# B's masks as a minimum on VectorE, early weights, held-back broadcasts and new planner weights in a two-part attention kernel

## Chip, cores, metric

One core of a Trainium2 chip runs the whole program in one launch. The metric is the device time of one execution in microseconds. Eight executions of the kernel before took 404.08 to 408.78 us, median 406.32.

## What is computed

Two independent attention layers over 2048 positions of 448 features, 16 heads of 28, concatenated:

```python
# A: one key/value head shared by 16 query heads, full softmax
q = (x @ wq).reshape(B, S, H, Dh).transpose(0, 2, 1, 3); k = x @ wk; v = x @ wv
p = softmax(einsum("bhqd,bkd->bhqk", q, k) * Dh ** -0.5)
a = einsum("bhqk,bkd->bhqd", p, v).transpose(0, 2, 1, 3).reshape(B, S, H * Dh) @ wo
# B: each position sees itself and 7 earlier ones at distance 2, 4, ..., 14
idx = pos[:, None] - arange(8)[None, :] * 2; mask = idx >= 0
logits = where(mask, einsum("bhsd,bhswd->bhsw", q, kg) * scale, -1e9)
b = (einsum("bhsw,bhswd->bhsd", softmax(logits), vg)).transpose(0, 2, 1, 3).reshape(B, S, D) @ wo
out = concatenate([a, b], axis=-1)
```

## The kernel before

A python planner (`plan`, `loop`) keeps a clock for each engine, asks for the next piece of work of the engine that is furthest behind, and writes down the instruction order of all five engines. Its costs, due times and thresholds are the constants at the head of the file. The program then runs those orders; a semaphore stands wherever an instruction needs another engine's result. So each engine runs strictly in the planned order, whatever the chip's true durations are.

**A.** The queries go by 16 groups (four chunks of 512 positions, four sets of four heads); each group has 64 jobs (16 blocks of 128 keys, four heads). A job is one QK matmul (`do_qk`, L1467) into a PSUM bank. Two rings of banks, three and two wide, alternate: ScalarE takes a ring with one exponential of 1536 or 1024 columns (L1214). Some jobs go by VectorE instead: a drain (`dread`, L1514) writes the score as an integer whose bits are a bf16 power of two, and two shifts (L1522, L1529), on VectorE or POOL, add three shifted copies that the PV products weigh. When no flexible bank is free, a job can be taken out of a three-wide ring. PV products (`do_pv`, L1577) run four at a time on column tiles of the array.

**B.** The positions are split by parity and half into four chunks, so that distance 2 becomes 1. Band matmuls of 32 keys by 25 queries (`b_fill`, L1310) write a bank; before them, four matmuls per bank (L1300) add a mask of 0 or -1e9 from `mask` through the identity. ScalarE takes each bank with one exponential (L1331), 16 in all; `bpv` (L1272) makes the PV products. Keys, queries and values come from `wB` and the transposed input `xT_B` (L654); values go through a scratch tensor in DRAM (`v_scratch`) into bands of 32.

**Fills.** Everything but QK and PV (projections, B's band matmuls, output projections) is a "fill", done in the order of its due time when TensorE has room before the next QK. `BT0` and `BDT` set B's due times. A dummy matmul is put in where TensorE would be too idle over a window (`HAMLOW`).

**Close of a group.** `chain` copies the PV bank (L980), moves the denominators by DMA, takes reciprocals (L996), writes them to DRAM, broadcasts them to 128 partitions with four DMAs on SP (`d3`), and multiplies on POOL (L1026). A's very last group is done on VectorE alone with two 32x32-block transposes (L950 to L971). When four groups of a chunk are ready, `outproj` runs 16 matmuls per 128 positions (`woA`, `woB`), copies the bank out (L1080 on ScalarE, L1082 on VectorE) and sends it by DMA.

**Start.** A's x chunk 0 is transposed on TensorE (L674); chunks 1 to 3 come by twelve DMA transposes on SP. Chunk 0's q (L654 on `wq`), its norm (a square on ScalarE, `sel`, an addition on VectorE, L755), k and v stand before the first QK. POOL builds constants and the mask, then issues the mask's copies, `wB` (as soon as k of chunk 0 is evicted), `woA` and `woB` (behind k of chunks 1 and 2). One DMA transpose of B's input is issued for every second exponential from the fourth on.

**Instruction fetch.** The planner assumes that TensorE's instructions arrive in blocks of 256 (`FBLOCK`, `block`, `fetched`) and keeps short matmuls away from a block that has not arrived.

Of the kernel before, what the change touches and what calls it, by code (L numbers as in the profile page):

```python
# [21 lines left out]
NEG = -1.0e9  # L22
# [35 lines left out]
BT0 = 98  # L58
BDT = 36
# [24 lines left out]
HAMLOW = 0.7  # L84
HAMTILE = 0.55
LATE = 1000.0
RINGD = 0.22
RINGB = 900.0
PRESS = 1
# [3 lines left out]
XL0 = 3600.0  # L93
FILLN = 130.0
FILL0 = 0.0
FRATE = 0.036

# [96 lines left out]
class _Gen:  # L194
# [297 lines left out]
    def plan_start(self):  # L492
# [29 lines left out]
        wA("act", g.wq, g.A_wq, D, "wq", 3800.0)  # L522
# [38 lines left out]
        for k in range(4):  # L561
# [6 lines left out]
                                     base=DH - 1, pattern=[[32, 4]], channel_multiplier=-1), 200, reads=[res("f2")], writes=[res("sel4")])  # L568
        gp(lambda e: e.memset(g.wB[0:64, 3, :], 0.0), 900, writes=[res("wB0")])
# [5 lines left out]
        gp(lambda e: e.memset(g.mask[0:32, :, :], 0.0), 450, writes=[res("m0")], name="band")  # L575

        def band(v, c0, n, rep, lo, rd, wr):
# [3 lines left out]
            gp(lambda e: e.affine_select(out=v, in_=v, compare_op=ALU.is_ge, fill=NEG, base=-lo, pattern=[[0, rep], [-1, n]],  # L581
                                         channel_multiplier=1), 270 + 2.0 * n * rep, reads=[rd], writes=[mid], name="band")
            gp(lambda e: e.affine_select(out=v, in_=v, compare_op=ALU.is_ge, fill=NEG, base=lo + HALO, pattern=[[0, rep], [1, n]],
# [6 lines left out]
        for s in range(1, 4):  # L590
            self.dma_op("gp", g.mask[32 * s:32 * s + 32, :, :], g.mask[0:32, :, :], reads=mres, writes=[res("mq", s)], issue=700.0, name="mq")
        self.mres = mres + [res("mq", s) for s in range(1, 4)] + [res("id")]
# [8 lines left out]
    def load_late(self, what):  # L601

        g = self
        res = self.res

        def dma(out, in_, reads, wr):
            def mk(eng, ns):
                return dict(dma=True, out=out, in_=in_, reads=reads, writes=[wr], lands=9000.0, moves=500.0)
            self.later(("gp",), (700,), reads, mk, prio=0, name="w")
        if what == 0:  # L610
            rd = [res("kA", 0), res("wB0")]
            dma(g.wB[:, 0:3, :], g.B_wqkv[0:384, :].rearrange("(k p) c -> p k c", p=128), rd, res("wB", 0))
            dma(g.wB[64:128, 3, :], g.B_wqkv[384:448, :], rd, res("wB", 1))
        else:
            t, src, key = ((g.woA, g.A_wo, "woA"), (g.woB, g.B_wo, "woB"))[what - 1]
            for j in range(4):
                dma(t[32 * j:32 * j + DH, :, :], src.rearrange("(t j d) c -> j d t c", j=4, d=DH)[j], [res("kA", what), res(key + "0")], res(key, j))

    def load_xb(self, exp):
# [9 lines left out]
        def mk(eng, ns):  # L629
            return dict(dma=True, transpose=True, out=g.xT_B[:, kt, 512 * c:512 * c + 512], in_=src, reads=[tick],  # L630
                        writes=[self.res("xB", c, kt)], lands=5500.0, moves=2000.0)
# [26 lines left out]
    def make_fills(self):  # L658
# [35 lines left out]
        for c in range(4):  # L694
# [7 lines left out]
            def after(bank, c=c):  # L702
# [3 lines left out]
                if c == 0:  # L706
                    self.evict(bank, lambda e: e.activation(kdst, ksrc, ACT.Identity, bias=g.col[:, 0:1]), ("act",), (480,),
                               reads=[res("c0")], writes=[res("kA", 0)], prio=0.5, name="ke", cb=lambda o: self.load_late(0))
# [3 lines left out]
                           prio=0.5 if c == 0 else 1, name="ke", cb=lambda o: self.load_late(c) if c < 3 else None)  # L712
# [143 lines left out]
        for b in range(16):  # L856
# [22 lines left out]
            fill(f"vB{b}", BT0 - 62 + 2.4 * b, steps, after, elig=30.0)  # L879
# [35 lines left out]
    def chain(self, key, bank):  # L915
# [93 lines left out]
        def d3(p, rk):  # L1009
# [6 lines left out]
            self.later(("sp",), (560,), [res("rd", rk)], mk, prio=0, gate=lambda: len(self.bcs.free) > 0, name="d3")  # L1016
# [111 lines left out]
    def loop(self):  # L1128
        guard = 0
        while self.nout < 32:  # L1130
            guard += 1
# [40 lines left out]
    def slot_free(self, slots, eng):  # L1172
        return len(slots.free) > 0 and self.ready(eng, [], [slots.res[slots.free[0]]]) <= self.T[eng] + 15.0

# [22 lines left out]
    def act_choose(self):  # L1197
# [3 lines left out]
        if self.actq:  # L1201
# [3 lines left out]
            if self.pslots.free and max(self.ready("act", [self.banks[b].res], []) for b in banks) <= T + 15.0:  # L1205
# [15 lines left out]
                if self.xbt and self.nexp >= 3 and self.nexp % 2 == 0:  # L1221
                    self.load_xb(op)
                return
# [66 lines left out]
    def b_fill(self, gg, j):  # L1290
# [5 lines left out]
        def steps(bank):  # L1296
            def mask(e):
                r = slice(32 * j, 32 * j + 32)
                for c in range(4):
# [470 lines left out]
```

## Time and profile before

| what | us |
|---|---|
| profiled execution, its own time | 404.08 |
| its span, first to last instruction | 402.3 |
| median of eight executions | 406.32 |
| ScalarE busy, of it A's exponentials (L1214) | 384.0, 371.6 |
| VectorE, POOL busy | 346.8, 130.0 |
| first exponential starts / last one ends | 10.49 / 389.80 |

The page gives for each engine the time in which it had an instruction, then groups of equal instructions with their count, busy time, mean length and the idle time before them. TensorE's matmuls overlap, so its busy share says less than the others'. The chain of waits follows the last instruction back to what released it. DMA queues: q1 is SP's, q10 ScalarE's, q0 POOL's, whose descriptors software writes; all share 16 DMA engines.

### The profile page before, as it was taken

The page shows a single profiled execution, that of the slowest core. Times are in us where ns is not written, and L with a number is a line of the kernel's source. Part 1 is how long each engine was busy: PE and PEld are TensorE (multiplying, and loading weights), DVE is VectorE, ACT ScalarE, POOL GpSimd, SP SyncE. Part 2 cuts the span into 40 slices and gives each one's busy share as a digit, 9 for nine tenths or more (in the row PEclk, how much of TensorE's full clock was granted, in tenths as well). Part 3 has the DMA queues.
Part 4 walks back from the last instruction along what each step waited for, and adds up shares of the span by engine and source line. Part 5 has one row for each costly group of instructions (what it writes and reads, how often), then busy time and mean ns, then how long its engine had stood idle before and what let it go on. Part 6 is the DMA issues. An engine that isn't in the chain of part 4 may idle for free.

```text
span 402.3 us, 16636 instructions
## 1 busy us (share of the span) xinstructions
PE 385.7 (96%) x7281; PEld 135.3 (34%) x7281; DVE 346.8 (86%) x803; ACT 384.0 (95%) x371; POOL 130.0 (32%) x165
## 2 busy tenths in 40 slices
PE   8897999999999999999999999999999999999995
PEld 4322222332233433222344333343333233333332
DVE  4886798889999999878999999899998878999832
ACT  3997999999999999999999999999999999999983
POOL 8830012733101021686101366420226611042510
PEclk9999999999999999999999999999999999999999
DMA  7699566424000022100001121100121210022404
GB/s 156 117 187 144 124 148 134 97 64 92 2 26 12 18 85 65 56 2 20 19 7 30 33 63 52 29 6 7 32 73 41 78 32 15 16 74 75 103 25 150
DMA packets 42532, 25.20 MB, mean 63 GB/s; under 512 B 28348, under 2 KB 37996, under 8 KB 42460
## 3 DMA queue, kind: packets, MB, share of 16 engines
q1 hardware_dynamic: 40332, 21.05, 23.3%
q0 software_dynamic: 736, 2.20, 2.9%
q8 instruction: 57, 0.93, 1.0%
q10 hardware_dynamic: 1392, 0.89, 0.8%
q14 instruction: 15, 0.12, 0.1%
HBM read 13.80 MB, written 6.02 MB: 49 GB/s over the span
## 4 chain that ended last, share of the span: by engine, by line
ACT 74%; PE 17%; DVE 5%; DMA 3%; issue 0%
ACT P L1214 72%; PE ps L1577 5%; PE ps L1467 4%; PE ps L654 3%; DMA xT_B<-in_B_x_dram 3%; DVE Z L1514 2%; ACT P L1331 1%; PE ps L1272 1%; PE ps L1310 1%; PE ps L596 1%; DVE Z L1529 1%; PE ps L674 0%; PE ps L1300 0%; DVE sq L1082 0%; DVE Z L1522 0%
## 5 line engine op out<-in xcount | busy, mean ns | idle before, releaser
L1214 ACT ACTIVATE P<-ps 128x1536 bf16<-128x1536 f32 (+1 forms) x341 | 371.6, 1271 | 4.6 <-PE ps L1467 4.5
L1514 DVE TENSOR_SCALAR Z<-ps 128x512 int16<-128x512 f32 x215 | 146.6, 686 | 20.0 <-PE ps L1467 18.7
L1577 PE MATMUL ps<-Z,vA 128*32 128x512 bf16 x860 | 143.8, 385 | 0.9 <-ACT P L1214 0.6
L1577 PE MATMUL ps<-P,vA 128*32 128x512 bf16 x809 | 139.0, 386 | 1.4 <-ACT P L1214 1.2
L1467 PE MATMUL ps<-qT_A,kT_A 29*128 29x512 bf16 x1024 | 133.7, 384 | 4.8 <-ACT P L1214 2.1
L1529 DVE TENSOR_SCALAR Z<-Z 128x1024 int16<-128x1024 int16 x173 | 77.3, 457 | 0.9
L1467 PEld LDWEIGHTS ps<-qT_A,kT_A 29*128 29x128 bf16 x1024 | 34.3, 91 | 120.1 <-ACT P L1214 59.3
L1026 POOL TENSOR_TENSOR oTn<-PVs,bc 128x512 bf16<-128x512 f32 x15 | 19.1, 1274 | 115.6 <-DVE Z L1522 54.9
L1522 POOL TENSOR_SCALAR Z<-Z 128x512 int16<-128x512 int16 x42 | 26.1, 624 | 84.9 <-DVE Z L1514 45.7
L1522 DVE TENSOR_SCALAR Z<-Z 128x512 int16<-128x512 int16 x173 | 47.9, 298 | 0.7
L1577 PEld LDWEIGHTS ps<-Z,vA 128*32 128x32 bf16 x860 | 35.3, 94 | 37.6 <-issue 22.4
L1577 PEld LDWEIGHTS ps<-P,vA 128*32 128x32 bf16 x809 | 34.2, 94 | 36.5 <-issue 20.9
L1529 POOL TENSOR_SCALAR Z<-Z 128x1024 int16<-128x1024 int16 x42 | 43.9, 1047 | 7.7 <-DVE Z L1529 4.0
L654 PE MATMUL ps<-xT_B,wB 128*32 128x512 bf16 x512 | 39.0, 382 | 0.0
L1026 POOL TENSOR_TENSOR oTnB<-PVs,bc 128x512 bf16<-128x512 f32 x16 | 20.4, 1272 | 35.9 <-DVE Z L1529 16.9
L980 DVE COPY PVs<-ps 128x512 f32<-128x512 f32 x31 | 21.2, 682 | 0.7 <-PE ps L1577 0.4
L654 PE MATMUL ps<-wB,xT_B 128*32 128x448 bf16 x256 | 18.6, 355 | 2.1 <-DMA xT_B<-in_B_x_dram 2.0
L654 PE MATMUL ps<-xT_A,wq 128*32 128x512 bf16 x256 | 19.4, 383 | 0.2
L654 PE MATMUL ps<-woA,oTn 128*32 128x448 bf16 x256 | 17.5, 355 | 0.0
L654 PE MATMUL ps<-woB,oTnB 128*32 128x448 bf16 x256 | 15.2, 353 | 0.0
L654 PEld LDWEIGHTS ps<-xT_B,wB 128*32 128x32 bf16 x512 | 10.6, 95 | 13.1 <-issue 6.3
L876 DVE CAST kT_B<-ps 128x448 bf16<-128x448 f32 x16 | 9.9, 620 | 5.9 <-PE ps L654 5.9
(100 smaller groups left out, 253.3 us busy)
## 6 DMA issues: line engine op xcount, KB each, us to landing
bc<-rec_scratch SPq DMA_DIRECT2D x124, 64.0 KB, 2.1
v_scratch<-kT_B SPq DMA_DIRECT2D x16, 128.0 KB, 3.6
out_dram<-sq SPq DMA_DIRECT2D x18, 112.0 KB, 2.1
out_dram<-ob SPq DMA_DIRECT2D x12, 112.0 KB, 2.4
vB<-v_scratch SPq DMA_DIRECT2D x2, 640.0 KB, 5.9
vB<-v_scratch SPq DMA_DIRECT2D x2, 608.0 KB, 6.1
wB<-in_B_wqkv_dram POOLq DMA_DIRECT2D x1, 1008.0 KB, 8.8
den<-PVs SPq DMA_DIRECT2D x31, 8.0 KB
```

The source lines that it names most:

```text
L596: self.pe_op("full", lambda e: e.matmul(g.bank(4), g.zero[:, 0:128], g.zero[:, :], start=True, stop=True), 430, reads=[res("zero")], write ...
L654: ins = e.matmul(self.bank(bank, 32 * j, 32 * j + m, 0, n), lhs(j), rhs(j), start=start, stop=stop, tile_position=(0, 32 * j))
L876: return dict(emit=lambda e: e.tensor_copy(out=g.vst[:, k, :, 0:DH], in_=g.bank(bank.i, 0, 128, 0, D).rearrange("p (h d) -> p h d", d=DH)) ...
L980: return dict(emit=lambda e: e.tensor_copy(out=g.PVs[:, p, :], in_=g.bank(bank.i)), reads=[bank.res], writes=[self.pvs.res[p]], took=ns + ...
L1026: return dict(emit=lambda e: e.tensor_tensor(out=dst(z), in0=g.PVs[:, p, :], in1=g.bc[:, b, :], op=ALU.mult), reads=[self.pvs.res[p], self ...
L1214: op = self.put("act", lambda e: e.activation(g.P[:, 1536 * k:1536 * k + 512 * n], g.ps[:, lo:lo + 512 * n], ACT.Exp, scale=ASCALE), ns, n ...
L1272: ins = e.matmul(g.bank(bank, 32 * j, 32 * j + 32, q0, n), g.vB[32 * c:32 * c + 32, b, 4 * gg + j, :], g.P[32 * c:32 * c + 32, x:x + n], s ...
L1467: ins = e.matmul(g.bank(b), g.kT_A[32 * j:32 * j + DH + 1, 128 * tb:128 * tb + 128], g.qT_A[32 * j:32 * j + DH + 1, gr.sc % 2, gr.g, :], s ...
L1514: return dict(emit=lambda e: e.tensor_scalar(out=g.Z[:, z, 0, :], in0=g.bank(bank.i), scalar1=ZBIAS, scalar2=0.0, op0=ALU.add, op1=ALU.max ...
L1522: return dict(emit=lambda e: e.tensor_scalar(out=g.Z[:, z, 1, :], in0=g.Z[:, z, 0, :], scalar1=1.0, scalar2=32.0, op0=ALU.mult, op1=ALU.ad ...
L1529: return dict(emit=lambda e: e.tensor_scalar(out=g.Z[:, z, 2:4, :], in0=g.Z[:, z, 0:2, :], scalar1=1.0, scalar2=64.0, op0=ALU.mult, op1=AL ...
L1577: ins = e.matmul(g.bank(b, 32 * j, 32 * j + 32), l, r, start=st, stop=sp, tile_position=(0, 32 * j))
```

## The change

1. B's mask is no longer added by matmuls. The mask tensor holds 3e38 inside the band and 0 outside, for the four chunks of a bank side by side; after each of B's exponentials VectorE takes the minimum of the result and the mask, in place. B's band matmuls start their own PSUM columns.
2. `wB` is fetched by POOL's queue right after the small constants, before POOL's memsets. `woA` and `woB` are fetched when exponentials 70 and 80 are planned. One transpose of B's input is issued for each exponential, and a transpose is planned to land sooner.
3. The broadcast DMAs (`d3`) are planned only while no block of TensorE's instructions is being fetched, and while the next is more than `FQUIET` instructions away.
4. Planner's constants: B's due times (`BT0` 87, `BDT` 38), landing times of the first loads, thresholds; and some of them change by stretches of planned time (`SCHED`).

```diff
-NEG = -1.0e9
+BIG = 3.0e38
-BT0 = 98
-BDT = 36
+BT0 = 87
+BDT = 38
-HAMLOW = 0.7
+HAMLOW = 0.5
-RINGD = 0.22
-RINGB = 900.0
-PRESS = 1
+RINGD = 0.25
+RINGB = 1200.0
+PRESS = 2
-XL0 = 3600.0
-FILLN = 130.0
-FILL0 = 0.0
+XL0 = 4300.0
+FILLN = 120.0
+FILL0 = 8.0
+FQUIET = 70
+SCHED = ((0, {'HAMLOW': 0.5, 'HAMTILE': 0.55, 'FILLN': 120.0, 'FILL0': 8.0, 'PV3': 8, 'RINGB': 1200.0, 'PRESS': 2, 'DWAIT': 100.0, 'FTOL': 250.0, 'TOL': 40.0, 'JOBO': 0.0, 'LATE': 1000.0, 'FSAFE': 300.0}),
+         (300, {'HAMLOW': 0.6, 'FTOL': 400.0, 'TOL': 20.0}),
+         (330, {'FTOL': 250.0, 'TOL': 40.0, 'LATE': -5.0}),
+         (355, {'HAMLOW': 0.5, 'FILL0': 4.0, 'RINGB': 1800.0, 'PRESS': 1, 'DWAIT': 300.0, 'LATE': 1000.0}),
+         (375, {'HAMLOW': 0.8, 'FILL0': 8.0, 'RINGB': 1200.0, 'PRESS': 2, 'DWAIT': 200.0}))
+VB0 = 27.0
+WO0 = 70
...
-        wA("act", g.wq, g.A_wq, D, "wq", 3800.0)
+        wA("act", g.wq, g.A_wq, D, "wq", 4500.0)
...
+        self.dma_op("gp", g.wB[:, 0:3, :], g.B_wqkv[0:384, :].rearrange("(k p) c -> p k c", p=128), writes=[res("wB", 0)], issue=700.0, lands=9000.0, name="w")
+        self.dma_op("gp", g.wB[64:128, 3, :], g.B_wqkv[384:448, :], writes=[res("wB", 1)], issue=700.0, lands=9000.0, name="w")
         gp(lambda e: e.memset(g.wB[0:64, 3, :], 0.0), 900, writes=[res("wB0")])
...
-            self.dma_op("gp", g.mask[32 * s:32 * s + 32, :, :], g.mask[0:32, :, :], reads=mres, writes=[res("mq", s)], issue=700.0, name="mq")
+            self.dma_op("gp", g.mask[32 * s:32 * s + 32, 0, :], g.mask[0:32, s % 2, :], reads=mres, writes=[res("mq", s)], issue=700.0, name="mq")
...
-                               reads=[res("c0")], writes=[res("kA", 0)], prio=0.5, name="ke", cb=lambda o: self.load_late(0))
+                               reads=[res("c0")], writes=[res("kA", 0)], prio=0.5, name="ke")
...
-                        writes=[self.res("xB", c, kt)], lands=5500.0, moves=2000.0)
+                        writes=[self.res("xB", c, kt)], lands=3500.0, moves=1300.0)
...
-            fill(f"vB{b}", BT0 - 62 + 2.4 * b, steps, after, elig=30.0)
+            fill(f"vB{b}", BT0 - 62 + 2.4 * b, steps, after, elig=VB0)
...
-            self.later(("sp",), (560,), [res("rd", rk)], mk, prio=0, gate=lambda: len(self.bcs.free) > 0, name="d3")
+            self.later(("sp",), (560,), [res("rd", rk)], mk, prio=0, gate=lambda: len(self.bcs.free) > 0 and self.quiet(), name="d3")
...
+            while sched and min(self.T.values()) >= 1000.0 * sched[0][0]:
+                globals().update(sched.pop(0)[1])
...
+    def quiet(self):
+
+        return self.T["sp"] >= self.fetched and FBLOCK * (self.block + 1) - self.ninst > FQUIET
...
-                if self.xbt and self.nexp >= 3 and self.nexp % 2 == 0:
+                if self.xbt and self.nexp >= 3:
                     self.load_xb(op)
+                if self.nexp in (WO0, WO0 + 10):
+                    self.load_late((self.nexp - WO0) // 10, op)
...
-            out = [("tile", mask, 217.0, self.mres, None, 0.47)]
+            out = []
...
-                                           g.qT_B[32 * j:32 * j + DH + 1, s, 512 * c + q0:512 * c + q0 + n], start=False, stop=(b == NB - 1),
+                                           g.qT_B[32 * j:32 * j + DH + 1, s, 512 * c + q0:512 * c + q0 + n], start=True, stop=True,
...
                 def cb(o):
-                    if j == 3:
-                        self.bpv(gg)
+                    def mk(eng, ns):
+                        return dict(emit=lambda e: e.tensor_tensor(out=g.P[:, x:x + 512], in0=g.P[:, x:x + 512], in1=g.mask[:, 0, :], op=ALU.min),
+                                    reads=[self.pslotres[k][j % 2]] + self.mres, writes=[self.pslotres[k][j % 2]], took=ns + 60, cb=lambda o: self.bpv(gg) if j == 3 else None)
+                    self.later(("dve",), (345,), [self.pslotres[k][j % 2]] + self.mres, mk, prio=1.25, name="min", port=True)
```

## The prediction

> **What bounds the kernel now.** I read the page's first and fourth part, then ScalarE's timeline, then the last 12 us of all engines, then DMA by stretch.
>
> ```profile
> span 402.3 us, 16636 instructions
> PE 385.7 (96%) x7281; PEld 135.3 (34%) x7281; DVE 346.8 (86%) x803; ACT 384.0 (95%) x371; POOL 130.0 (32%) x165
> ACT 74%; PE 17%; DVE 5%; DMA 3%; issue 0%
> L1214 ACT ACTIVATE P<-ps 128x1024 bf16<-128x1024 f32 x214 | 222.3, 1115 | 0.0
> L1214 ACT ACTIVATE P<-ps 128x1536 bf16<-128x1536 f32 x127 | 194.7, 1533 | 4.6 <-PE ps L1467 4.5
> ```
>
> TensorE looks as busy as ScalarE, but its matmuls overlap; the chain of waits names ScalarE for 74%. The two groups are the exponentials of A (two or three PSUM banks each). So the sum has four terms: the start of the first exponential, the exponentials, ScalarE's stalls between them, and what follows the last.
>
> ```profile
> 10.49 6.89 ACT L1214 ACTIVATE P<-ps 128x1536 bf16<-128x1536 f32 x6 [1.16 <-PE ps L1467]
> 17.60 15.94 ACT L1214 ACTIVATE P<-ps 128x1536 bf16<-128x1536 f32 x14 [0.23 <-PE ps L1467]
> 35.99 4.63 ACT L1214 ACTIVATE P<-ps 128x1536 bf16<-128x1536 f32 x4 [2.46 <-PE ps L1467]
> 379.30 10.50 ACT L1214 ACTIVATE P<-ps 128x1536 bf16<-128x1536 f32 x9
> ```
>
> Columns: start, length, count, idle before. Three-bank and two-bank instructions alternate. The second row is eight instructions longer than the first: 9.05 us for four pairs, 2.26 a pair. The last holds five of three banks and four of two: 10.50 less four pairs and 0.1 of drain leaves 1.35 for three banks, so 0.91 for two. (The group means of 1533 and 1115 ns include the overlap with the next.) The first starts at 10.49, the last ends at 389.80. The one large stall is 2.46 us at 33.5. Its cause, from the chain and from DMA by stretch (6 to 10 us, then 20 to 26):
>
> ```profile
> 25.02 10.18 DMA xT_B<-in_B_x_dram
> q1 hardware_dynamic: 1899, 0.45, 65.2%
> q0 software_dynamic: 292, 1.28, 97.8%
> q1 hardware_dynamic: 403, 0.10, 9.5%
> ```
>
> A transpose of B's input took 10.18 us to land because POOL's queue (q0) was fetching B's weights, issued at 18.4, and the two output weights: the transposes' queue (q1) fell from 475 packets a us to 67. The tail:
>
> ```profile
> 390.29 0.72 DVE L950 STREAM_TRANSPOSE PVs<-ps 128x512 f32<-128x512 f32 x1 [6.10 <-PE ps L1577]
> 392.82 0.94 PE L654 MATMUL ps<-woA,oTn 128*32 128x448 bf16 x16
> 393.59 4.33 PE L654 MATMUL ps<-woB,oTnB 128*32 128x448 bf16 x88
> 397.98 0.54 ACT L1080 ACTIVATE sq<-ps 128x448 bf16<-128x448 f32 x1 [0.21 <-PE ps L654]
> ```
>
> After the last exponential the chain of A's last group needs until 393.76, but 88 matmuls of B's output projection still stand behind it; the last copy ends at 398.52 and the span at 402.34.
>
> **The change, part by part,** against this execution: 404.08 us, 1.78 outside its span. It is the fastest of the eight; the median is 406.32, so 2.24 is added at the end, taking the scatter to stay.
>
> *Tail.* In the changed order 16 matmuls of woB, not 144, stand behind the last exponential, and all of them ahead of A's last 16. With E its end: last PV products E+0.45 (389.85 to 390.25 before), DVE's four steps 2.48 (390.29 to 392.77), A's 16 matmuls 0.94, last copy 0.6, and from there 3.8 to the end, as before (398.52 to 402.34). That is E+8.4 for E+12.5. **-4.0** (-2.5 to -4.6; the low end if the last group but one comes late through SP's queue). The 20 dummies at the very end lie under the output DMAs.
>
> *Exponentials.* The order has 111 of three banks and 239 of two, for 127 and 214: -16 x 1.35 + 25 x 0.91 = **+1.2**. Two fewer jobs go by VectorE (213 drains, L1514, for 215). ScalarE's copies in the tail fall from 9 to 3; they are in the tail's sum.
>
> *First exponential.* The order puts the 16 k matmuls ahead of the 16 q matmuls (before: q at 6.67, k at 7.55). Three of four k slots run while ScalarE still copies x, so Square moves from 7.77 by about 0.7; VectorE then does the norm's addition ahead of v's transpose, which returns about 0.15. **+0.55** (0.3 to 0.9).
>
> *Weights of B early.* Two DMAs (1008 and 168 KB) go on POOL's queue at about 4.3 us (after L567), some 1.35 us of issue (18.42 to 19.76); POOL's memsets, selects and mask copies behind them wait that long and are not needed for 80 us. The fetch now meets the twelve transposes of A's x. Worse, TensorE's order has the four k steps of chunk 1, each waiting on one transpose, right behind the first two groups of QK (five matmuls, two exponentials) and eight q matmuls, ahead of the third group; before, they stood one or two groups later. Rows: the fourth transpose is issued near 6.2 and lands 3.1 later undisturbed; at 1.28 MB in 6 us the fetch takes 5.5, until 11.5 to 12. Here stands a rule against the change, from the Trainium skill, DMA: Bandwidth & Descriptors, section "Queues, rings and completion order": each DMA engine takes turns between queues packet by packet. The row bears it out (403 packets beside 292 much larger ones). By the rule, the transposes stand still as long as the fetch flows and then catch up: the fourth lands near 13.4, the third group ends near 14.05, and ScalarE, fed by two exponentials until 11.05 + 2.26 = 13.3, loses 0.8. By the row of B's transposes (landing 14.1 us at the worst) it lands near 20.3 and the loss is 7.7. There up to 2.1 MB was queued, with small packets of woA and woB behind wB; here 1.18. I take **+0.8** (0 to 7.7).
>
> *B's transposes.* They are issued after each exponential from 18.5 on, with nothing on POOL's queue but half the mask; woA and woB wait for exponentials 70 and 80 (each 4 x 0.6 us of POOL, near 90 and 100 us, where POOL is idle 7 to 9 tenths). The first v step of B stands behind the 16th group of QK, near 28; four transposes at 1.3 plus 3.1 land near 27. Most of the 2.46 goes, and the tiles that would be late next are chunk 1's, with 2 us to spare: **-2.3** (0 to -2.6).
>
> *Broadcasts apart from fetches.* One row shows what it aims at:
>
> ```profile
> 149.20 0.37 PE L1467 MATMUL ps<-qT_A,kT_A 29*128 29x512 bf16 x1 [0.73 <-issue]
> ```
>
> A QK stalls 0.73 us in mid-group with no semaphore to wait for, while SP issues broadcasts. **-0.7** (0 to -0.9). A broadcast held back delays only A's and B's normalisation, which has several us everywhere but in the tail.
>
> *Masks.* Off TensorE: 16 steps of four matmuls, 0.22 each, 3.5 us. Onto VectorE: 16 minimums; the nearest row is a bf16 tensor_tensor of this size (L817, 417 ns): 6.7 us. VectorE loses 18 pairs of shifts (298 + 457 ns, 13.6 us) to POOL and gains six copies (3.7), so it ends 3 lower; POOL's 16 more pairs (0.62 + 1.05) add 27 to 130. Queued behind a minimum on VectorE are drains and shifts, 0.4 us later; B's PV fills wait for it, but TensorE's order has other work there. TensorE saves 3.5 on masks and 11 groups of dummies (0.19 each, 2.1) ahead of the last exponential, and gets 27 output-projection steps (0.19, 5.1), nine more QK (0.22, 2.0) and 19 more mode switches (about 0.1, 2.0): **3.5 us more**, inside some 25 of slack. **+0.5** (-1.5 to +3.5): small stalls of 0.15 to 0.4 us a dozen times are in the trace now, and the slack is thinner.
>
> Sum: -4.0 + 1.2 + 0.55 + 0.8 - 2.3 - 0.7 + 0.5 = -3.95. Span 398.35, profiled time 400.1, **median 402.4 us**.
>
> **Rivals.**
> A. The head eats half: the fourth transpose lands near 16.5 and the loss is 3.9, not 0.8: 405.5, no change that can be told (0.5% is 2 us, about what a measurement here can tell). For it: transposes starved in 20 to 33 us even where q0 moved only 0.51 MB. Against: that was traffic in small packets, gone here.
> B. **Slower.** TensorE stands in order on the k steps of chunk 1 while the fetch starves the transposes as it did B's. Landing after 14.1: loss 7.7 for 0.8, and SP, whose issues took up to 4.66 us in that jam, hands on B's transposes late, so the 2.3 is not gained: 411.6. It turns the sign from a fourth landing later than 17.3. For it: the 14.1 row. Against: less is queued.
> C. TensorE takes over: its 3.5 us more all show, and POOL's longer shifts (1.05 us for 0.46) make PV wait: 405.5 with all of the upper bound. Against: ScalarE is 20.00 of 20 busy in most stretches with slack on PE; and the exponentials keep their place in the order.
> That the tail doesn't shrink is not a rival: its order is fixed in the program.
> The granted clock was 1.00 in every stretch; with fewer dummies a long wait in the head could lower it, which goes with B.
>
> **Chances.** Forecast 0.66, A 0.12, C 0.09, B 0.13. The forecast's own range is 399 to 405; most of it, and a little of A and C, is faster by over 0.5% (below 404.3): 0.67. Same: 0.19. Slower: 0.14. The range leaves out B and a thin edge below: 398.5 to 407.5.
>
> **What would show it.** Tail: the end 8 to 9 us after the last exponential, woA's 16 matmuls last. Head: first exponential near 11.05; a stall before the third of 0 to 2 us, released by a DMA of xT_A. No DMA of xT_B on the chain near 33 us. No issue wait over 0.5 on a QK. Between 40 us and the last exponential, ScalarE's idle time no larger than now. A stall over 5 us near 13 would prove B; many small stalls at B's stages, C.

## The result, and the profile after

The changed kernel takes **401.66 us** (median of 20 runs, 400.55 to 405.78); the kernel before, run beside it, 406.95 (57 runs, 402.04 to 412.82). The ratio is 0.9906, 95% interval 0.9883 to 0.9929: 0.9% faster, with a median of 402.4 predicted. The ratio leaves out runs more than 1.5% above the fastest of their kernel, so it lies nearer to 1 than the 0.987 of the two medians. The profiled execution took 402.02 us, its span 400.2. The medians lie 5.3 us apart, the profiled executions only 2.1: the sum of the prediction was made on the profiles, and there it was too good.

The page of the kernel after, first part (busy time) and the first line of the chain of waits:

```profile
span 400.2 us, 16464 instructions
PE 385.3 (96%) x7178; PEld 134.8 (34%) x7178; DVE 350.8 (88%) x787; ACT 381.7 (95%) x374; POOL 156.4 (39%) x197
ACT 76%; PE 13%; DVE 6%; DMA 3%; SPq 1%; issue 1%
```

ScalarE is still the bound. TensorE's busy time is where it was (385.3 for 385.7); VectorE has 4 us more, where the prediction had it 3 lower, and POOL 26 more, as predicted. A's exponentials by shape, from the groups of instructions (count, then busy time, mean ns, idle before):

```profile
L1227 ACT ACTIVATE P<-ps 128x1024 bf16<-128x1024 f32 x239 | 243.6, 1127 | 1.1 <-PE ps L1479 1.1
L1227 ACT ACTIVATE P<-ps 128x1536 bf16<-128x1536 f32 x111 | 171.9, 1549 | 3.2 <-PE ps L1479 3.2
```

From start to start two of them are usually 0.904 us (two banks) and 1.330 us (three) apart, in both traces. That cuts each span into four terms:

| us | before | after | difference |
|---|---|---|---|
| first exponential starts ("first" below) | 10.49 | 11.65 | +1.16 |
| A's exponentials, 0.904 and 1.330 each | 362.37 | 363.69 | +1.32 |
| the rest between first and last (stalls, B's 16 exponentials; "rest") | 16.94 | 15.38 | -1.56 |
| from the last one's end to the end of the span ("tail") | 12.54 | 9.47 | -3.07 |

ScalarE's timeline after (start, length, line and operation, count, idle before and who ended it):

```profile
8.97 0.60 ACT L838 ACTIVATE sq<-ps 128x512 bf16<-128x512 f32 x1 [0.18 <-PE ps L662]
11.65 2.37 ACT L1227 ACTIVATE P<-ps 128x1536 bf16<-128x1536 f32 x2 [2.08 <-PE ps L1479]
15.13 32.78 ACT L1227 ACTIVATE P<-ps 128x1536 bf16<-128x1536 f32 x29 [1.12 <-PE ps L1479]
48.97 11.47 ACT L1227 ACTIVATE P<-ps 128x1024 bf16<-128x1024 f32 x11 [1.06 <-PE ps L1479]
```

The 2.46 us before 35.99 are gone: from 15.13 the exponentials run 32.78 us without a gap that the view shows. Two new stalls stand beside that, 1.12 us before 15.13 and 1.06 before 48.97. For the first, the chain of waits (first fence) and TensorE's timeline (second) name a transpose of A's x:

```profile
4.95 8.96 DMA xT_A<-in_A_x_dram
```

```profile
13.95 0.81 PE L662 MATMUL ps<-xT_A,wk 128*32 128x512 bf16 x8 [1.17 <-DMA xT_A<-in_A_x_dram]
```

The third transpose of A's x, issued at 4.95, landed at 13.91, just after `wB` (13.72). DMA by stretch, 6 to 10 us, shows what it shared the engines with; each line is a queue with its packets, MB and share of the 16 engines:

```profile
q0 software_dynamic: 215, 1.09, 102.2%
q1 hardware_dynamic: 580, 0.14, 23.7%
```

Before, q1 moved 1,899 packets in this stretch. The second new stall was not foreseen. VectorE's timeline:

```profile
47.34 0.25 DVE L1004 RECIPROCAL rec<-den 128x16 f32<-128x16 f32 x1 [1.36 <-DMA den<-PVs]
```

The first group's denominators were ready for their DMA at 42.3 us; SP issued it at 45.40, behind two transposes of B's input and two stores of values, because the starved transposes of the head had held SP up (one issue took 2.94 us) and it was some 2 us late with everything. VectorE stood in order behind the reciprocal, QK behind VectorE, ScalarE behind QK. The new order has a part in this: before, the same DMA was also issued 1.5 us after its source was ready (43.53), but VectorE's order had the reciprocal 4.5 us behind its landing (45.44, 49.95).

At the end, TensorE's timeline after the last exponential (which ends at 390.71):

```profile
392.87 0.94 PE L662 MATMUL ps<-woB,oTnB 128*32 128x448 bf16 x14
393.74 0.94 PE L662 MATMUL ps<-woA,oTn 128*32 128x448 bf16 x16
```

`woA`'s 16 come last, as the order said, and 16 of `woB` instead of 144 stand there. But behind the last copy (395.34) come 4.84 us, not 3.8. SP's waits from 387 us on (line waited at, who ended it: total, times, longest):

```profile
SPq L413 <- DMA out_dram<-sq: 2.0, 1, 2.0
```

SP waits at the end of the program for 56 semaphores, one after another. The one of the last landing, released at 397.69, comes early in that order; then SP goes through the others, two to an instruction, an instruction each 0.061 us, until 399.74, though they were all there long before.

### The profile page after: what moved, and what is told of

Its sections match the earlier page's. It is cut to its first block, busy times and chain, and to the rows that moved or that the text cites. A ratio compares the mean times of both kernels' runs of the same rounds, so it can differ in the third digit from the quotient of the medians.

```text
span 400.2 us, 16464 instructions
## 1 busy us (share of the span) xinstructions
PE 385.3 (96%) x7178; PEld 134.8 (34%) x7178; DVE 350.8 (88%) x787; ACT 381.7 (95%) x374; POOL 156.4 (39%) x197
## 4 chain that ended last, share of the span: by engine, by line
ACT 76%; PE 13%; DVE 6%; DMA 3%; SPq 1%; issue 1%
ACT P L1227 74%; PE ps L1589 4%; PE ps L662 4%; PE ps L1479 4%; DMA xT_A<-in_A_x_dram 2%; DVE Z L1526 2%; ACT P L1343 2%; DVE Z L1541 1%; SPq L333 1%; DVE Z L1534 1%; DVE sq L1090 1%; DMA den<-PVs 0%; DVE ob L1090 0%; PE ps L1672 0%; DVE PVs L988 0%
## 5 line engine op out<-in xcount | busy, mean ns | idle before, releaser
L1526 DVE TENSOR_SCALAR Z<-ps 128x512 int16<-128x512 f32 x213 | 144.5, 684 | 19.2 <-PE ps L1479 18.0
L1589 PE MATMUL ps<-Z,vA 128*32 128x512 bf16 x852 | 145.7, 385 | 1.4 <-DVE Z L1526 0.7
L1589 PE MATMUL ps<-P,vA 128*32 128x512 bf16 x811 | 146.0, 386 | 0.9 <-ACT P L1227 0.4
L1479 PE MATMUL ps<-qT_A,kT_A 29*128 29x512 bf16 x1024 | 136.8, 384 | 4.4 <-DVE Z L1526 1.2
L1534 POOL TENSOR_SCALAR Z<-Z 128x512 int16<-128x512 int16 x58 | 36.0, 622 | 144.4 <-DVE Z L1541 64.1
L1479 PEld LDWEIGHTS ps<-qT_A,kT_A 29*128 29x128 bf16 x1024 | 35.2, 90 | 119.8 <-ACT P L1227 51.7
L1541 DVE TENSOR_SCALAR Z<-Z 128x1024 int16<-128x1024 int16 x155 | 72.8, 477 | 0.8
L1541 POOL TENSOR_SCALAR Z<-Z 128x1024 int16<-128x1024 int16 x58 | 60.6, 1046 | 11.8 <-DVE Z L1541 5.6
L1589 PEld LDWEIGHTS ps<-P,vA 128*32 128x32 bf16 x811 | 36.6, 94 | 36.1 <-issue 19.7
L1034 POOL TENSOR_TENSOR oTnB<-PVs,bc 128x512 bf16<-128x512 f32 x16 | 20.3, 1272 | 31.6 <-DVE Z L1541 18.2
L662 PE MATMUL ps<-woB,oTnB 128*32 128x448 bf16 x256 | 18.2, 355 | 0.0
L662 PEld LDWEIGHTS ps<-xT_B,wB 128*32 128x32 bf16 x512 | 10.8, 95 | 13.4 <-issue 6.3
L1287 PE MATMUL ps<-P,vB 32*32 32x25 bf16 (+1 forms) x1344 | 15.1, 171 | 0.0
```

Of the source, the lines that this page charges most:

```text
L662: ins = e.matmul(self.bank(bank, 32 * j, 32 * j + m, 0, n), lhs(j), rhs(j), start=start, stop=stop, tile_position=(0, 32 * j))
L1034: return dict(emit=lambda e: e.tensor_tensor(out=dst(z), in0=g.PVs[:, p, :], in1=g.bc[:, b, :], op=ALU.mult), reads=[self.pvs.res[p], self ...
L1287: ins = e.matmul(g.bank(bank, 32 * j, 32 * j + 32, q0, n), g.vB[32 * c:32 * c + 32, b, 4 * gg + j, :], g.P[32 * c:32 * c + 32, x:x + n], s ...
L1479: ins = e.matmul(g.bank(b), g.kT_A[32 * j:32 * j + DH + 1, 128 * tb:128 * tb + 128], g.qT_A[32 * j:32 * j + DH + 1, gr.sc % 2, gr.g, :], s ...
L1526: return dict(emit=lambda e: e.tensor_scalar(out=g.Z[:, z, 0, :], in0=g.bank(bank.i), scalar1=ZBIAS, scalar2=0.0, op0=ALU.add, op1=ALU.max ...
L1534: return dict(emit=lambda e: e.tensor_scalar(out=g.Z[:, z, 1, :], in0=g.Z[:, z, 0, :], scalar1=1.0, scalar2=32.0, op0=ALU.mult, op1=ALU.ad ...
```

## The experiments

All ratios are to the kernel before, run beside each; the last three columns are the terms of the table above, from each run's profiled execution. In e1 to e4 and p1 the profiled time lies above the median, so rest and tail are somewhat longer than they would be at the median.

| run | median (range, runs) us | profiled | ratio, 95% | first | rest | tail |
|---|---|---|---|---|---|---|
| e1_wb_behind_mask | 405.03 (401.56-409.73, 9) | 408.24 | 0.9944 (0.9904-0.9984) | 11.2 | 22.0 | 9.5 |
| e2_no_quiet | 409.00 (407.36-412.98, 11) | 412.98 | 1.0083 (1.0055-1.0110) | 11.0 | 24.4 | 13.7 |
| e3_old_weights | 411.69 (410.93-414.02, 4) | 414.02 | 1.0171 (1.0120-1.0221) | 10.2 | 21.0 | 14.7 |
| e4_final_sorted | 400.58 (398.21-401.91, 4) | 401.91 | 0.9880 (0.9826-0.9934) | 11.6 | 17.0 | 7.8 |
| e5_den_first | 400.83 (400.11-404.02, 4) | 400.38 | 0.9878 (0.9818-0.9938) | 11.5 | 13.8 | 9.5 |
| e6_v_first | 402.18 (399.45-405.65, 4) | 400.40 | 0.9864 (0.9796-0.9933) | 11.6 | 13.8 | 9.5 |
| e8_min_tiny | 401.87 (400.97-402.52, 4) | 400.97 | 0.9878 (0.9847-0.9909) | 11.2 | 14.8 | 9.5 |
| p1_placebo | 441.84 (440.06-447.54, 4) | 443.43 | 1.0847 (1.0788-1.0906) | 11.6 | 18.2 | 49.8 |
| b1_wo_late | 401.98 (401.01-405.75, 16) | 401.82 | 0.9908 (0.9878-0.9938) | 10.2 | 14.9 | 12.6 |
| b2_wo_late_finals_early | 400.70 (399.05-405.56, 6) | 399.37 | 0.9886 (0.9817-0.9954) | 10.4 | 14.0 | 10.9 |
| c1_three_mends | 399.55 (398.37-401.64, 6) | 398.37 | 0.9846 (0.9792-0.9899) | 11.2 | 14.1 | 7.6 |
| c2_and_q_first | 398.45 (398.10-399.17, 6) | 398.46 | 0.9817 (0.9764-0.9871) | 12.2 | 13.1 | 7.6 |

Most of these keep the planned order of every engine and move single instructions in the finished list, by a method called between planning and the placing of semaphores. Where the planner runs anew (e2, e3, p1), the whole order changes.

**The early fetch, undone in the new order.**

```diff
+        wb = [o for o in self.ops if o.eng == "gp" and o.dma and o.name == "w"][:2]
+        rest = [o for o in self.ops if o not in wb]
+        at = max(i for i, o in enumerate(rest) if o.name == "mq") + 1
+        self.ops = rest[:at] + wb + rest[at:]
```

> The changed kernel with the same planned order on every engine, but the two DMAs of wB stand on POOL's queue behind the mask's copies (near 18 us, as before the change) instead of at 4.2 us. Theory (the early fetch starves A's DMA transposes and makes SP late): the 1.12 us stall of ScalarE before its third exponential goes to under 0.3, the transposes of A's x land within 4 us each, and the stall of 1.1 us near 47 us (reciprocals waiting for a denominator DMA that SP issued late) is gone; in exchange B's transposes are starved again and ScalarE stalls 1 to 3 us between 28 and 40 us. Sum 400.5 to 403.5 profiled, for 402.0. Rival (the planned order alone makes these stalls): the stalls before the third exponential and near 47 us stay at 1.1 us each, and the new stall comes on top: 403.5 to 405.

Both stalls of the theory vanished. The exchange was dearer than thought: `wB`, now issued at 17.64, caught the last transpose of A's x (issued 18.18, landed 28.47) and ScalarE stood 6 us:

```profile
30.14 1.02 ACT L1237 ACTIVATE P<-ps 128x1024 bf16<-128x1024 f32 x1 [6.07 <-PE ps L1489]
```

What followed was new. By stretches of 2 us: length, TensorE's busy time and matmuls, **granted clock**, DMA share, GB/s:

```profile
22.00:24.00 2.00, 0.49 (x8) 1.00 1.61 251
24.00:26.00 2.00, 0.00 (x0) 0.84 0.75 74
26.00:28.00 2.00, 0.00 (x0) 0.50 1.30 72
28.00:30.00 2.00, 1.49 (x10) 0.50 1.04 208
...
38.00:40.00 2.00, 2.00 (x29) 0.75 0.20 66
```

TensorE stood from 22.49 to 28.51. Its clock was halved from 25.36 and stayed so until 39.02, some 10 us after TensorE worked again; small stalls of ScalarE (0.50, 0.56, 1.30 us) followed in that time. With all this the profiled time, 408.24, lies 3.2 us above e1's median.

**The broadcasts' condition, taken away:**

```diff
-            self.later(... gate=lambda: len(self.bcs.free) > 0 and self.quiet(), name="d3")
+            self.later(... gate=lambda: len(self.bcs.free) > 0, name="d3")
```

> The changed kernel without the condition that holds broadcasts back from instruction fetches; the planner runs anew, so other things move a little. Theory (the condition removes fetch stalls): QK matmuls with an idle time of over 0.5 us put down to issue come back, and the time rises by 0.7 to 1.5 us: about 403 profiled, median 402.5 to 403. Rival (it does nothing that can be told): none of these rows, within 0.5 us of the changed kernel's 401.7.

**The old constants in the changed kernel** (and so on for HAMLOW, RINGD, RINGB, PRESS, XL0, FILLN, FILL0, VB0):

```diff
-BT0 = 87
-BDT = 38
+BT0 = 98
+BDT = 36
...
-        sched = list(SCHED)
+        sched = []
```

> The changed kernel with the planner's constants of before (B's due times, thresholds, first landing times, no stretches) and all the rest of the change kept. Theory (the constants shortened the tail): some hundred matmuls of B's output projection stand behind the last exponential again, the span ends about 12.5 us after it instead of 9.5, and the first exponential starts near 10.5 instead of 11.65: +3 -1.1, about 404 profiled, median 403.5 to 405. Rival (the masks and the early fetch carry the gain): a time within 0.5 us of 401.7, with the tail near 9.5 us.

The theory of the condition falls as it was put: without the condition no `issue` wait of 0.4 us or more stands in TensorE's timeline, and with it, in e3, one of 0.74 us does, in the middle of B's band matmuls. Both were slower by more than either theory said, and mostly in other places than the parts they undo: e2's profile has 4.9 us more of ScalarE's stalls from 40 to 61 us, 2.7 more near 208, and 4.2 more of tail; e3's 5.6 between the exponentials, 2.6 in their number, 5.2 of tail. Part of that is the clock: it was at 0.50 from 48.77 to 59.01 in e2's profile, from 16.09 to 22.92 and from 275.50 to 278.91 in e3's. It is not all: e2's runs with a mean clock of 0.998 or more still took 407.4 to 408.3. e3's tail is as its theory had it, with 96 matmuls of `woB` last. Whether such a difference belongs to the part or to the new order was then the question, and so a constant was moved that has no part in the change:

```diff
-EXP0 = 52.0
+EXP0 = 53.0
```

> The changed kernel with one cost of the planner that has nothing to do with the change moved by 1 ns (the fixed part of an exponential, 52 to 53 ns); the planner then decides anew from about 10 us on, and by its own clock this order ends its last exponential 0.9 us earlier than the changed kernel's. Theory (the changed kernel's constants were fitted to the chip for just this order, so that any other order that the same rules give is worse): 404 to 409, as without the broadcasts' condition (409.0), and that run then says little of the condition. Rival (orders of the same rules are worth the same): 400.5 to 402.5.

One nanosecond costs 40 us. Up to the last exponential this order is nearly as good as the changed kernel's (it ends at 391.56 for 390.71); all of it is tail, where all of B's output projection and a part of its PV were left. TensorE's groups from 392 us on:

```profile
L1672 PE MATMUL ps<-wq 128*32 128x448 bf16 x554 | 29.4, 353 | 0.6 <-issue 0.6
L662 PE MATMUL ps<-woB,oTnB 128*32 128x448 bf16 x256 | 13.5, 352 | 0.0
```

(L1672 are dummies.) So one order came out well with these constants, and a run with a new plan cannot by itself say what a single part does: e2 and e3 leave open what the condition and each constant do. From here on only finished lists were edited.

**The final waits in the order of landing**

```diff
-                    for k, v in final.items():
-                        eng.wait_ge(dsem[k], v)
+                    last = {d.dsem: d.done for d in ends}
+                    for k in sorted(final, key=lambda k: last[k]):
+                        eng.wait_ge(dsem[k], final[k])
```

> The changed kernel with the same order everywhere; only SP's 56 waits at the very end, one for each semaphore of an output or scratch DMA, are put in the order in which their DMAs are planned to land. Theory (SP goes through the waits one by one at 0.061 us each, and some 34 of them stand behind the one that is released last): the span ends within 0.6 us of the last landing instead of 2.5 behind it: -2.0 us, 400.0 profiled, median 399.6. Rival (what follows the last landing is a fixed cost of closing the program): no change, 401.7.

The tail fell by 1.70 us, and SP's waits show how; the line answers to the one of 2.0 us above:

```profile
SPq L414 <- DMA out_dram<-sq: 0.2, 1, 0.2
```

The 28 instructions now run while the last outputs are still under way. The profiled time (401.91) hid it, for the stall near 46 us was 2.4 us long in that execution, and again the clock, by stretches of 1 us:

```profile
46.00:47.00 1.00, 0.56 (x10) 1.00 0.47 140
47.00:48.00 1.00, 0.00 (x0) 1.00 0.21 41
48.00:49.00 1.00, 0.03 (x3) 1.00 0.58 53
...
50.00:51.00 1.00, 1.00 (x11) 0.53 1.16 231
...
53.00:54.00 1.00, 1.00 (x9) 0.76 0.61 174
```

TensorE had no matmul for 2.4 us (46.56 to 48.97); a us after it had resumed, its clock was halved for 3.41 us, and ScalarE lost another 1.4 us waiting. Where the same stall was 1.2 us, in the changed kernel's own profile, the clock stayed at 1.00. The Trainium skill (TensorE: Matmul & The Clock Gate, section "Part 1: The HAM clock gate (the "warmup" mystery)") says that the clock goes to half after about one idle window of 3.4 us, and that the window runs freely. Half is what the rows show, and every stretch at half in these traces is a multiple of 3.41 us long (3.41 here; 13.65 in e1, 10.24 in e2, 6.83 and 3.41 in e3, 6.83 in p1), as a window of that length would make it. But a gap of 2.41 us was enough here, where by the rule one of under 3.4 might pass. A gap's length alone does not decide: in p1 one of 1.40 us at the same place (46.86 to 48.26) was followed by 6.83 us at half, in e2 one of 1.62 (12.18 to 13.79) by none. So much the same stall costs 1 us in one execution and several in another; what decides is not shown.

**The denominators ahead in SP's queue**

```diff
+        d1 = next(o for o in self.ops if o.eng == "sp" and o.name == "d1")
+        at = self.ops.index(d1)
+        back = [o for o in self.ops[:at] if o.eng == "sp"][-4:]
+        back = [o for o in back if o.name == "xBt"][-1:] + [o for o in back if o.name == "vs"][-1:]
+        rest = [o for o in self.ops if o not in back]
+        at = rest.index(d1) + 1
+        self.ops = rest[:at] + back + rest[at:]
```

> The changed kernel, same order but for SP's queue at 41 us: the denominators' DMA of the first group stands ahead of one transpose of B's input and one store of values instead of behind them. Theory (the stall near 46 us comes from this DMA alone, whose source is ready at 42.3 us and which SP issues at 45.4; where TensorE then stands for over 2 us its clock falls for some us, and this makes part of the scatter): the reciprocal no longer waits, ScalarE's stall near 46 us goes from 1.2 to under 0.3, profiled time 400.8, median 399.5 to 400.8, and no run over 404. Rival (SP is late anyway and the two that move back are then waited for): the stall moves by a few us and stays, 401.5 to 402.5.

Issued at 42.56 and landed at 44.48 (the reciprocal, at 44.85, no longer waits), and ScalarE runs through:

```profile
39.03 22.37 ACT L1240 ACTIVATE P<-ps 128x1536 bf16<-128x1536 f32 x21
```

The rest between the exponentials fell by 1.5 us and the profiled span to 398.5. One of four runs was at 404.02 (mean clock 0.991), so this stall is not all of the scatter; that it is a part of it, four runs cannot show.

**A third of the early fetch** (wB's two DMAs split by columns; those of q and k go behind 58 us on POOL):

```diff
+        for c0, c1, key in ((2 * D, 3 * D, "wBv"), (0, 2 * D, "wB")):
+            self.dma_op("gp", g.wB[:, 0:3, c0:c1], g.B_wqkv[0:384, c0:c1].rearrange("(k p) c -> p k c", p=128), writes=[res(key, 0)], issue=350.0, lands=9000.0, name=key)
...
+        wb = [o for o in self.ops if o.name == "wB"]
+        rest = [o for o in self.ops if o not in wb]
+        at = next(i for i, o in enumerate(rest) if o.eng == "gp" and o.start > 58000.0)
+        self.ops = rest[:at] + wb + rest[at:]
```

> The changed kernel, same order, but only the value columns of wB (0.40 of 1.18 MB) are fetched at 4.2 us; the query and key columns, first read at 82 us, are fetched by POOL near 58 us. Theory (the size of the early fetch sets how long A's transposes stand still): the fourth transpose lands near 11.5 to 12 instead of 14.3, the stall of 1.12 us before the third exponential falls under 0.4, SP issues the transposes of B some 2 us earlier, and the stall near 46 us shrinks with it: -1.0 to -2.0, profiled 400.2 to 401.0, median 399.8 to 400.7. Rival (a packet of a software queue takes its turn whatever the size, or smaller packets of 896 bytes cost as much as those of 2,688): fourth transpose after 13.5, no gain.

The fourth transpose landed at 10.23, q1 moved 2,081 packets between 6 and 10 us, and the third exponential waits no more:

```profile
11.58 34.95 ACT L1239 ACTIVATE P<-ps 128x1536 bf16<-128x1536 f32 x31 [2.08 <-PE ps L1491]
47.16 13.30 ACT L1239 ACTIVATE P<-ps 128x1024 bf16<-128x1024 f32 x13 [0.63 <-PE ps L1491]
```

SP issued the denominators at 43.61 instead of 45.40, and what is left of the second stall is 0.63 us. So it is the early fetch that starves the transposes, and less of it does not; whether by its amount or by its shorter rows, both of which changed, this run does not separate. Of the gain expected in the median nothing shows: 402.18, with two of the four runs at 403.96 and 405.65 (mean clock 0.995 and 0.989).

**The minimum itself**

```diff
-    ... e.tensor_tensor(out=g.P[:, x:x + 512], in0=g.P[:, x:x + 512], in1=g.mask[:, 0, :], op=ALU.min) ...
+    ... e.tensor_tensor(out=g.P[:, x:x + 8], in0=g.P[:, x:x + 8], in1=g.mask[:, 0, 0:8], op=ALU.min) ...
```

> The changed kernel, same order, but each of B's 16 minimums covers 8 columns instead of 512, so that most of B's mask is left out (B's outputs then take in keys outside the window). It prices the minimum itself on VectorE. Theory (VectorE has slack where they stand): 16 x about 0.35 us less on VectorE (350.8 to 345) and no change that can be told, 0 to -0.5 us, 401.4. Rival (B's bands wait for VectorE and the minimums are on the path): -2 to -5 us, with less idle time of ScalarE around 180 to 300 us.

16 of 468 ns became 16 of 192 ns, VectorE's busy time fell by 4 us, and the time did not move: the minimum's length is free where it stands.

**One part of the change, alone, in the order of before**

```diff
+        wo = [o for o in self.ops if o.eng == "gp" and o.dma and o.name == "w"][2:]
+        rest = [o for o in self.ops if o not in wo]
+        at = next(i for i, o in enumerate(rest) if o.eng == "gp" and o.start > 54000.0)
+        self.ops = rest[:at] + wo + rest[at:]
```

> The kernel before, same order, one part of the change alone: the eight DMAs of woA and woB go out on POOL's queue near 54 us instead of from 19.8 us on; wB stays at 18.4 us. Theory (the small packets of the output weights behind wB prolong the starving of B's transposes, and the stall that follows is what makes TensorE's clock fall in part of the runs): the fourth transpose of B lands near 31 instead of 35.2, ScalarE's stall of 2.46 us before 36 us goes, profiled 401.5 to 402.5, and the median comes down by more than the profile, by 3 to 4 us, to a ratio near 0.991. Rival (wB alone starves them): the stall stays over 1.5 us and the time within 1 us of before.

**This is the main finding.** Eight DMAs moved by 36 us (`woA` is first read at 126 here) give 0.9908 with an interval of 0.9878 to 0.9938, the whole change 0.9906. The transposes of B land at 27.2 to 29.2 us instead of 32.7 to 35.2, and ScalarE has no gap there:

```profile
17.25 43.14 ACT L1224 ACTIVATE P<-ps 128x1536 bf16<-128x1536 f32 x39 [0.16 <-PE ps L1477]
```

DMA from 20 to 26 us, where `wB` is fetched as before but with nothing behind it:

```profile
q0 software_dynamic: 246, 1.15, 58.1%
q1 hardware_dynamic: 568, 0.13, 33.1%
```

With the output weights behind it, q0 had held 97.8% of the engines' time there and q1 9.5%. The profile gained 2.3 us of span, the median 4.8: 11 of its 16 runs lie between 401.0 and 402.1 us with a mean clock of 0.996 or more, while the runs of before beside them reach from 403.06 (0.997) to 409.77 (0.982): the six of these 21 with 0.994 or more took 403.06 to 405.89, the ten with 0.989 or less 406.68 to 409.77.

**What can be mended, together.** c1 joins e5 and e6 and puts the final waits where SP stands idle:

```diff
+                tail = lists[name][-3]
...
+                    if name == "sp" and o is tail:
+                        for d in [d for d in final.values() if d.idx < tail.idx]:
+                            eng.wait_ge(dsem[d.dsem], d.dval)
+                            final.pop(d.dsem)
```

> The changed kernel with three mends of what the traces showed, same planned order: only wB's value columns at 4.2 us (the rest near 58 us), the first denominators' DMA ahead of a transpose and a store, and SP's final waits for all DMAs but the last few put ahead of its last three DMAs, where it stands idle from 388.8 to 394.4 us. Theory: the three add up, because they lie at different places: stalls before the third exponential and near 46 us gone (-2.3), end within 0.7 us of the last landing (-1.9): profiled 397.8 to 398.3, median 397 to 398.5, ratio near 0.978. Rival (each frees only what the next limit takes back): 399 to 400, no better than the best of the three alone.

c2 also moves chunk 0's k matmuls and their copy:

```diff
+        k0 = [o for o in self.ops if o.name == "k0"] + [next(o for o in self.ops if o.name == "ke")]
+        sq = next(o for o in self.ops if o.name == "sq")
+        rest = [o for o in self.ops if o not in k0]
+        at = rest.index(sq) + 1
+        self.ops = rest[:at] + k0 + rest[at:]
```

> As the version with three mends, and chunk 0's 16 q matmuls ahead of its 16 k matmuls again, as before the change. Theory (the order k before q costs the first exponential 0.6 to 1.1 us, which was hidden by the stall before the third exponential and is on the path once that is gone): first exponential at 10.6 to 11.0 instead of 11.6, and the whole 0.6 to 1.0 us less than the version with three mends: median 396.3 to 397.8. Rival (the third exponential then waits for the transposes of A's x again): no difference.

In c1's profile (398.37) both stalls are gone; 49 us pass from the first exponential without a visible gap:

```profile
11.20 49.49 ACT L1251 ACTIVATE P<-ps 128x1536 bf16<-128x1536 f32 x45 [2.08 <-PE ps L1503]
```

But the parts did not add up as expected, and the profile lies near the range by other terms. The rest is 14.07, no less than with e5 or e6 alone (13.84, 13.83), because a third stall of the same kind stands behind the two:

```profile
71.10 0.25 DVE L1028 RECIPROCAL rec<-den 128x16 f32<-128x16 f32 x1 [1.15 <-DMA den<-PVs]
72.88 3.28 ACT L1251 ACTIVATE P<-ps 128x1024 bf16<-128x1024 f32 x3 [0.97 <-PE ps L1503]
```

The second group's denominators took 4.23 us to land (66.84 to 71.07; 1.87 in the changed kernel), beside the part of `wB` that was moved here (landed at 69.83) and B's value bands. With the same move they took 2.94 in e6 and 2.49 in c2, without it 2.07 in e5, so the moved fetch is the likely cause. The tail gave 1.9 us, and the first exponential came 0.45 earlier because the copy of x on ScalarE did (6.23 for 6.67). The median, 399.55, is 1 us above what was expected and in the rival's range; the ratio is 0.9846 for 0.978.

In c2 the reason failed. From ScalarE's copy of x to the first exponential it takes 5.02 us, in c1 4.97: the square comes sooner after that copy, but in this order the norm's matmul takes the PSUM bank that k's copy frees, and that copy, at 9.65, was now behind the square. That the first exponential stands at 12.22 is the later copy of x in this execution (7.20). The rest shrank by the same us, since the stall near 73 us is not there, and the profiles end alike (396.6 and 396.5). That c2 has the lowest median of all, 398.45, its interval does not separate from c1.

**The early waits in the order of before** (b1's edit, and that of c1 with another place):

```diff
+                tail = lists[name][-11]
```

> The kernel before, same order, with the output weights fetched near 54 us (as in the run that moved them alone) and SP's final waits for all DMAs but the last eleven put ahead of these, where SP stands idle from 381 to 389 us. It asks what the new order (masks, planner's constants) is worth when loads and final waits are mended in both programs. Theory (the new order is worth its tail less its own costs: 3.1 of tail, less 1.3 of exponentials and 1.0 of a later first exponential, plus 0.9 of smaller stalls): tail 12.6 to 10.8, span 398.2 to 398.5, profiled 400.0 to 400.3, median 399.8 to 400.8, that is 1 to 2 us above the changed kernel with three mends. Rival (the final waits cost nothing in this program, whose last copies are 0.75 us apart): the time of the run that moved the output weights alone, 402.

The tail fell from 12.6 to 10.9, so the final waits are on the path in this program too. b2 lies 1.1 us above c1 in median and in span: that is what the rest of the change (masks, constants, broadcasts) would be worth once loads and final waits are mended in both. The intervals of the two ratios overlap, so that it is worth anything is not shown.

## Why the prediction was right, and where it was not

The median (402.4 for 401.66), the sign and the forecast's own range held, the median by two errors that nearly cancel. By the steps:

- **B's transposes, -2.3: right.** The stall went (2.65 us more than the usual distance before, nothing after), and b1 shows the cause, the weights of the output behind `wB`.
- **Tail, -4.0: right in mechanism, -3.07 in size.** VectorE's four steps, the last 16 matmuls and the last copy came as summed (the last copy's end at E+4.63 for E+4.47; with the 3.8 behind it the prediction's own terms make E+8.27, not 8.4). The term that was mis-sized is "from there 3.8 to the end, as before": it was 4.84. It was taken for fixed, and was a landing (2.35 us after the copy for 1.74) and a queue of semaphore waits (2.5 us for 2.1).
- **Exponentials, +1.2: right** (+1.32).
- **First exponential, +0.55: +1.16.** The square moved by 1.20 us (7.77 to 8.97), not 0.7. It waited for the last q matmul (8.95 for 7.75), 0.18 us longer than for k's copy, which stands ahead of it on ScalarE: two of k's four slots, not three, ran while ScalarE copied x, and a dummy stands between them and the others. From the copy of x on it is +1.08; the start of that copy shifts by up to 0.5 us among runs of this order.
- **Early weights, +0.8: +1.1 and more.** By the rule of turns packet by packet, as taken, the fourth transpose was to land near 13.4; it did at 14.31. The rule was taken too strictly: taking turns does not make the transposes stand still, and 580 of their packets passed beside 215 of the fetch. The step did not follow the delay along SP's queue: it cost another 1.2 us near 46 us, where the prediction had looked only at B's transposes, and not at what else stands in order on SP.
- **Broadcasts, -0.7: the row is gone, the reason not shown.** e2 lost the row without the condition, e3 has one with it.
- **Masks and TensorE's slack, +0.5: about -0.5.** That is what is left of the rest without the four named stalls (each over the usual distance: before 2.65 and 0.89, after 1.23 and 1.21): 13.40 before, 12.94 after. e8 prices the minimum's length at nothing. VectorE did not end 3 us lower but 4 higher: the minimum took 468 ns for 417, and the shifts grew by 34 and 20 ns, over 155 pairs some 8 us by these means; it cost nothing that shows.

The sum on the profile was -3.95 and came out at -2.06. What made the median right all the same is the last step, which **failed**: "2.24 is added at the end, taking the scatter to stay". It did not stay; the changed kernel's median lies 0.4 us below its profile instead of 2.24 above. An error of 1.9 against the forecast and one of 2.6 for it nearly cancelled, which is luck. The runs put in its place: the long stall of the head was not worth 2.5 us, as the profile of the fastest execution had it, but about 5 in the median, since a stall that leaves TensorE without work can be followed by half its clock for some us, and for how long differs from run to run. That the halvings of before sat at that stall is argued from e1 and e4, and from b1's scatter; no profile of a scattered run of before was taken, and in the one there is, TensorE's gaps at that stall are 0.76 and 0.80 us and the clock stays at 1.00.

Of the rivals, A saw the right place (transposes of A starved) and put 3.9 us on it; 1.1 was the wait itself. B's mechanism did come, in e1 and not in the change: a transpose that landed 10.3 us after its issue, 6 us of stall, the clock with it. C did not come: what small stalls there are did not grow.

## What to carry to other kernels

Before rewriting an order, look at which transfer stands in the queues behind the one that is waited for: moving eight loads that nothing reads before 125 us gave as much as the whole change. Price a stall of TensorE by the median of several runs, not by the one profiled, when the granted clock differs between runs; and where a planner decides, test a part on the finished order, with a placebo beside every new plan. A load that is moved out of one stage's way can stand in another's: look there too.

## What the runs showed of the hardware

- SP goes through semaphore waits that are long satisfied at 0.061 us an instruction of two; 28 of them at the end of a program are 1.7 us, on the path unless they stand ahead of the last landing.
- TensorE's clock, gap without a matmul and time at half that followed: 6.03 and 13.65 us (e1), 2.41 and 3.41 (e4), 2.14 and 10.24 (e2), 1.89 and 6.83 (e3), 1.40 and 6.83 (p1); nothing after 1.62 (e2), nor after 1.17 and 1.18 (changed kernel).
- 1.09 MB on a software queue left DMA transposes 580 packets where they had 1,899; with 0.40 MB they had 2,081 in the same 4 us.
- VectorE's shifts of 128x1024 that ran while POOL had an instruction took 709 ns on average in the changed kernel (32 of 155), the others 416; of 128x512, 560 (28) and 281. That makes the means of 477 and 332 ns, 457 and 298 before, where 25 and 13 of 173 met POOL.
